# Residual by identity matmul, ScalarE copy and ScalarE's own queue for the last output piece

## The chip, the cores and the metric

The kernel runs on one core of one Trainium2 chip. The metric is the device time of one execution in microseconds (us). A profile gives the span of the core, from its first to its last instruction. This is about 2 us less than the device time.

## The reference, cut to what matters

Two layer types take turns, twice each, on x of 2048 rows by 1024 columns in bf16. The change touches the end of the last one:

```python
def _B_ref(x, w_gate, w_up, w_down):
    g = jnp.einsum("bsd,df->bsf", x, w_gate)
    u = jnp.einsum("bsd,df->bsf", x, w_up)
    h = g * u
    return jnp.einsum("bsf,fd->bsd", h, w_down)
...
x = x + _B_ref(_layernorm(x, axis=-1), B_w_gate, B_w_up, B_w_down)
```

The result is the residual x plus a down projection with an inner size of 3584. The kernel does this for 16 row tiles of 128 rows, each as a sum of 28 products of 128 by 128 weights (KF = 28).

## The kernel before

The residual lies in SBUF in `X`, in bf16, for all row tiles. Fifteen row tiles are finished whole (`d_unit`). The last is finished in three column pieces, so that only the small third piece has its addition and store after TensorE's last product:

```python
def add_store(t, a, b, ps, last):
    nc.vector.tensor_tensor(out=X[:, t, a:b], in0=X[:, t, a:b], in1=ps, op=ALU.add)
    if last:
        nc.sync.dma_start(out=o_view[:, t, a:b], in_=X[:, t, a:b])
...
def d_end(t):
    def run():
        tl = t % TPG
        for a, b in ((0, 512), (512, 896), (896, 1024)):
            ps = mm_tile()
            for f in range(KF):
                nc.tensor.matmul(out=ps[:, 0, 0:b - a], lhsT=hT[:, f, tl * P:(tl + 1) * P], rhs=wd[f][:, a:b],
                                 start=(f == 0), stop=(f == KF - 1))
            add_store(t, a, b, ps[:, 0, 0:b - a], True)
    return run
```

`mm_tile` hands out one of three accumulators in PSUM. `ident` is a 128 by 128 identity in bf16, made at the start for transposes. A pool of three small buffers (`eb`) is used by ScalarE's copies.

Of the kernel before, what the change touches and what calls it, by code (L numbers as in the profile page):

```python
# [11 lines left out]
BF16 = mybir.dt.bfloat16  # L12
# [14 lines left out]
def kernel(  # L27
# [11 lines left out]
    nc = tc.nc  # L39
    P = 128  # L40
    S, D = A_x.shape[1], A_x.shape[2]
# [3 lines left out]
    KF = F // P  # L45
# [10 lines left out]
    small = ctx.enter_context(tc.tile_pool(name="small", bufs=4))  # L56
# [8 lines left out]
    X = const.tile([P, NT, D], BF16, tag="X", name="X")  # L65
# [33 lines left out]
    o_view = out[0].rearrange("(t p) d -> p t d", p=P)  # L99
# [48 lines left out]
    ident = const.tile([P, P], BF16, tag="ident", name="ident")  # L148
# [6 lines left out]
    def mm_tile():  # L155
        return psum.tile([P, 2, NB], F32, tag="mm", bufs=3, name="ps")
# [388 lines left out]
# [4 lines that stand above are left out]
# [10 lines left out]
    def d_end(t):  # L559
        def run():  # L560
            tl = t % TPG
            for a, b in ((0, 512), (512, 896), (896, 1024)):
                ps = mm_tile()
                for f in range(KF):
                    nc.tensor.matmul(out=ps[:, 0, 0:b - a], lhsT=hT[:, f, tl * P:(tl + 1) * P], rhs=wd[f][:, a:b],  # L565
                                     start=(f == 0), stop=(f == KF - 1))
                add_store(t, a, b, ps[:, 0, 0:b - a], True)
        return run

    def do(units):  # L570
# [82 lines left out]
```

## Time and profile before

| | before |
|---|---|
| time, median of 3 runs (lowest to highest) | 1622.09 us (1621.53 to 1622.28) |
| span of the profiled run | 1620.1 us |
| TensorE busy | 1607.5 us, 99% |
| VectorE / ScalarE busy | 38% / 18% |
| end of TensorE's last product to end of span | some 2.65 us |

Read it from the end. The chain that ended last is TensorE's for 99% of the span, so nothing on another engine costs time unless TensorE waits for it, or it comes after TensorE's last product. The last three rows of the chain, in order of time (start, length, what):

```profile
1614.88 2.55 PE ps L565 x34
1617.44 0.02 issue
1617.46 0.29 DVE X L546
```

The add of 0.29 us is the only computation left after TensorE. The store and the closing barrier follow it.

### The profile page before, as it was taken

What the parts mean: (1) busy time and instruction counts of PE and PEld (TensorE: products, weight loads), DVE (VectorE), ACT (ScalarE), POOL (GpSimd) and SP (SyncE); (2) the same over time, 40 slices, a digit from 0 to 9 for tenths busy, and PEclk for the clock granted to TensorE, in tenths of its full rate; (3) what the DMA queues carried; (4) which work ended last, traced back from release to release, by engine and by line L of the source; (5) the groups of instructions that cost most, each with busy time, mean ns of one, the idle gap of its engine ahead of it and who ended that gap; (6) DMA issues with size and microseconds to landing.
All of it is one profiled execution on the core that took longest, in us unless ns stands there. A gap on an engine that the chain in (4) does not pass through costs nothing.

```text
span 1620.1 us, 18047 instructions
## 1 busy us (share of the span) xinstructions
PE 1607.5 (99%) x7710; PEld 734.5 (45%) x7861; DVE 616.6 (38%) x946; ACT 284.0 (18%) x384; POOL 54.5 (3%) x135
## 2 busy tenths in 40 slices
PE   9999999999999999999999999999999999999999
PEld 4444444444444444444444444444444444444444
DVE  6899853202311321243255798432123113211111
ACT  5522201101110110011045231011011101101110
POOL 2100000000000000010000000000000000000000
DMA  8224856512650552142420257655236306521400
GB/s 247 53 72 93 246 162 176 162 52 60 171 159 0 147 162 81 52 156 66 92 52 1 78 114 219 181 157 165 69 102 175 127 20 173 165 66 65 156 1 26
DMA packets 236719, 183.10 MB, mean 113 GB/s; under 512 B 102368, under 2 KB 217312, under 8 KB 236640
## 3 DMA queue, kind: packets, MB, share of 16 engines
q1 hardware_dynamic: 236640, 181.95, 39.0%
q8 instruction: 61, 1.00, 0.3%
q14 instruction: 18, 0.15, 0.0%
HBM read 153.09 MB, written 4.19 MB: 97 GB/s over the span
## 4 chain that ended last, share of the span: by engine, by line
PE 99%; issue 1%; DMA 0%; SPq 0%; DVE 0%
PE ps L196 50%; PE ps L538 48%; PE ps L565 1%; DMA W<-in_A_wqkv_dram 0%; PE kv L306 0%; SPq L109 0%; PE pm L328 0%; PE ps L328 0%; DVE X L546 0%
## 5 line engine op out<-in xcount | busy, mean ns | idle before, releaser
L538 PE MATMUL ps<-xT,R 128*128 128x512 bf16 x2382 | 525.9, 379 | 2.6
L538 PEld LDWEIGHTS <-R 128*128 128x128 bf16 x2432 | 238.0, 98 | 286.9
L542 DVE TENSOR_TENSOR R<-gs,ps 128x512 bf16<-128x512 f32 x224 | 153.9, 687 | 533.5 <-ACT gs L541 533.5
L196 PEld LDWEIGHTS <-R 128*128 128x128 bf16 x2248 | 220.0, 98 | 265.2
L541 ACT COPY gs<-ps 128x512 f32<-128x512 f32 x224 | 131.3, 586 | 1040.2 <-PE ps L538 1011.5
L538 PE MATMUL ps<-xT,W 128*128 128x512 bf16 x1130 | 250.4, 379 | 1.2
L196 PEld LDWEIGHTS <-xT 128*128 128x128 bf16 x1536 | 149.5, 98 | 181.4 <-issue 1.9
L196 PE MATMUL ps<-W,xT 128*128 128x512 bf16 x997 | 222.8, 379 | 1.9 <-issue 0.3
L538 PEld LDWEIGHTS <-W 128*128 128x128 bf16 x1152 | 112.7, 98 | 135.9
L196 PE MATMUL ps<-W,R 128*128 128x512 bf16 x733 | 170.1, 379 | 0.8
L546 DVE TENSOR_TENSOR X<-X,ps 128x1024 bf16<-128x1024 bf16 (+3 forms) x34 | 39.4, 1158 | 335.8 <-PE ps L196 282.8
L196 PE MATMUL ps<-R,R 128*128 128x512 bf16 x506 | 111.8, 379 | 0.4
L196 PE MATMUL ps<-PQ,R 128*128 128x512 bf16 x488 | 111.4, 379 | 0.5
L196 PE MATMUL ps<-R,xT 128*128 128x512 bf16 x502 | 110.3, 379 | 0.5
L201 ACT ACTIVATE e<-ps 128x1024 bf16<-128x1024 f32 x56 | 57.3, 1024 | 141.2 <-PE ps L196 86.0
L175 DVE BATCH_NORM_STATS2 st<-X 128x6 f32<-128x512 bf16 x128 | 81.7, 680 | 0.1
L179 POOL TENSOR_SCALAR ve<-mv 128x1 f32<-128x1 f32 x64 | 16.2, 254 | 1325.8 <-DVE mv L177 1325.8
L196 PE MATMUL ps<-GL,R 128*128 128x512 bf16 x240 | 57.8, 379 | 0.3
L196 PE MATMUL ps<-xT,R 128*128 128x512 bf16 x240 | 57.5, 379 | 0.2
L378 DVE TENSOR_TENSOR X<-X,ps 128x1024 bf16<-128x1024 bf16 x32 | 38.7, 1209 | 17.0 <-PE ps L196 17.0
L186 DVE TENSOR_SCALAR R<-X,mv,rstd 128x1024 bf16<-128x1024 bf16 x64 | 33.7, 542 | 27.3 <-POOL rstd L181 24.0
L205 DVE TENSOR_SCALAR e<-e 128x1024 bf16<-128x1024 bf16 x64 | 26.9, 421 | 38.1 <-ACT e L201 38.1
(73 smaller groups left out, 456.6 us busy)
## 6 DMA issues: line engine op xcount, KB each, us to landing
R<-in_B_w_gate_dram SPq DMA_DIRECT2D x38, 1024.0 KB, 5.4
R<-in_B_w_up_dram SPq DMA_DIRECT2D x38, 1024.0 KB, 7.6
W<-in_B_w_gate_dram SPq DMA_DIRECT2D x18, 1024.0 KB, 5.4
W<-in_B_w_up_dram SPq DMA_DIRECT2D x18, 1024.0 KB, 7.6
W<-in_A_wqkv_dram SPq DMA_DIRECT2D x10, 1024.0 KB, 6.2
W<-in_B_w_down_dram SPq DMA_DIRECT2D x6, 1024.0 KB, 11.2
X<-in_A_x_dram SPq DMA_DIRECT2D x16, 256.0 KB, 6.7
PQ<-in_B_w_down_dram SPq DMA_DIRECT2D x4, 1024.0 KB, 8.4
```

Of the source, the lines that this page charges most:

```text
L175: nc.vector.bn_stats(out=st[:, c, :], in_=X[:, t, c * NB:(c + 1) * NB])
L179: nc.gpsimd.tensor_scalar(out=ve[:], in0=mv[:, 1:2], scalar1=1e-5, scalar2=None, op0=ALU.add)
L186: nc.vector.tensor_scalar(out=dst, in0=X[:, t, :], scalar1=mv[:, 0:1], scalar2=rstd[:], op0=ALU.subtract, op1=ALU.mult)
L196: nc.tensor.matmul(out=ps[:, n, :], lhsT=lhsT, rhs=rhs[:, n * NB:(n + 1) * NB], start=start, stop=stop)
L201: nc.scalar.activation(out=e[:], in_=flat(ps), func=ACT.Exp, **sc)
L205: nc.vector.tensor_scalar(out=e[:], in0=e[:], scalar1=1.0, scalar2=EPS, op0=ALU.min, op1=ALU.add)
L378: nc.vector.tensor_tensor(out=X[:, t, :], in0=X[:, t, :], in1=flat(ps), op=ALU.add)
L538: nc.tensor.matmul(out=ps[:, n, :], lhsT=w[:, k, j * P:(j + 1) * P], rhs=xT[g % 2][:, k, :], start=(k == 0), stop=(k == KD - 1))
L541: nc.scalar.copy(out=gs[:], in_=ps[:, 0, :])
L542: nc.vector.tensor_tensor(out=hT[:, f, :], in0=gs[:], in1=ps[:, 1, :], op=ALU.mult)
L546: nc.vector.tensor_tensor(out=X[:, t, a:b], in0=X[:, t, a:b], in1=ps, op=ALU.add)
L565: nc.tensor.matmul(out=ps[:, 0, 0:b - a], lhsT=hT[:, f, tl * P:(tl + 1) * P], rhs=wd[f][:, a:b], start=(f == 0), stop=(f == KF - 1))
```

## The change

The intent is to shorten this tail. The residual of the third piece enters the accumulator through TensorE, so no addition is left; ScalarE, idle by then, takes the sum out; and the store is issued by the same engine, without a hand-over to SyncE. The result is rounded to bf16 once in both versions.

```diff
             for a, b in ((0, 512), (512, 896), (896, 1024)):
                 ps = mm_tile()
+                last = b == D
+                if last:
+
+                    nc.tensor.matmul(out=ps[:, 0, 0:b - a], lhsT=ident[:], rhs=X[:, t, a:b], start=True, stop=False)
                 for f in range(KF):
                     nc.tensor.matmul(out=ps[:, 0, 0:b - a], lhsT=hT[:, f, tl * P:(tl + 1) * P], rhs=wd[f][:, a:b],
-                                     start=(f == 0), stop=(f == KF - 1))
-                add_store(t, a, b, ps[:, 0, 0:b - a], True)
+                                     start=(f == 0 and not last), stop=(f == KF - 1))
+                if last:
+                    o = small.tile([P, P], BF16, tag="eb", bufs=3, name="o")
+                    nc.scalar.copy(out=o[:], in_=ps[:, 0, 0:b - a])
+                    nc.scalar.dma_start(out=o_view[:, t, a:b], in_=o[:])
+                else:
+                    add_store(t, a, b, ps[:, 0, 0:b - a], True)
```

## The prediction

> **What bounds the kernel now.** I read the page's list of busy engines first, then the chain that ended last, and then, because the change touches only the last 128 columns of the last row tile, the timeline, the waits and the issues of the last 16 us.
>
> ```profile
> span 1620.1 us, 18047 instructions
> PE 1607.5 (99%) x7710; PEld 734.5 (45%) x7861; DVE 616.6 (38%) x946; ACT 284.0 (18%) x384; POOL 54.5 (3%) x135
> PE 99%; issue 1%; DMA 0%; SPq 0%; DVE 0%
> PE ps L196 50%; PE ps L538 48%; PE ps L565 1%; DMA W<-in_A_wqkv_dram 0%; PE kv L306 0%; SPq L109 0%; PE pm L328 0%; PE ps L328 0%; DVE X L546 0%
> ```
>
> TensorE holds the chain from one end to the other. VectorE (38%), ScalarE (18%) and the transfers hang beside it. The changed function is the source line 565 group, 1% of the chain. So whatever is done to the last piece can only move what comes after TensorE's last product, plus any matmul put into its stream. The timeline of the end shows the size of that:
>
> ```profile
> 1615.70 0.61 PE L565 MATMUL ps<-PQ,R 128*128 128x128 bf16 x8
> 1615.90 0.56 DVE L546 TENSOR_TENSOR X<-X,ps 128x384 bf16<-128x384 bf16 x1 [3.86 <-PE ps L565]
> 1616.14 0.61 PE L565 MATMUL ps<-W,R 128*128 128x128 bf16 x8
> 1616.59 0.39 PE L565 MATMUL ps<-GL,R 128*128 128x128 bf16 x4
> 1616.81 0.39 PE L565 MATMUL ps<-W,R 128*128 128x128 bf16 x4
> 1617.04 0.39 PE L565 MATMUL ps<-xT,R 128*128 128x128 bf16 x4
> 1617.46 0.29 DVE L546 TENSOR_TENSOR X<-X,ps 128x128 bf16<-128x128 bf16 x1 [1.01 <-PE ps L565]
> ```
>
> Columns: start, duration, engine, line, operation, count, and the idle time ahead. The last matmul ends about 1617.43 (1617.04 + 0.39), the add runs 1617.46 to 1617.75 (it is 288 ns), and the store is issued at once. The views of the store and of the closing line read:
>
> ```profile
> 1617.78 0.33 SPq L548 DMA_DIRECT2D out_dram<-X  x1
> out_dram<-X SPq DMA_DIRECT2D x1, 32.0 KB, 1.5
> SPq L648 <- DMA out_dram<-X: 0.9, 1, 0.9
> L648 SPq EVENT_SEMAPHORE  x7: 17/28/28, 1618.2 to 1620.0; - x7
> ```
>
> Issue at 1617.78, landing 1.5 us later, near 1619.28. SyncE has by then waited 0.9 us for it, and the closing barrier takes the 0.8 us to 1620.1. The whole tail after TensorE is 1620.1 - 1617.43 = 2.67 us: 0.03 hop, 0.29 add, 0.03 hop, 1.5 store, 0.8 barrier (these make 2.65). It is 0.16% of the time. **Even removing the add entirely could not make a difference of 2%**, which is 32 us.
>
> **What the Trainium skill says.** *TensorE: Matmul & The Clock Gate*, "Back-to-back issue gap", gives an isolated warm 128-column matmul 134 cycles (55.8 ns at its 2.4 GHz), and about 81 ns where every matmul has its own weight load. The trace: 24 starts from 1615.70 to 1617.04 make 1.34/24 = 55.8 ns each, weight loads included. It agrees with the first number and not with the second, so I use 56 ns.
>
> *ScalarE: Activation LUTs*, "What ACT_TABLE_LOAD costs", gives 186 ns + 0.833 ns per column for an ACTIVATE with immediate scale and bias. In the trace a copy out of PSUM takes 586 ns for 512 columns (line 541) and 1012 ns for 1024 (line 296): slope 426/512 = 0.832, fixed part 160 ns. The slope agrees, the fixed part is 26 ns lower for a copy. At 128 columns the trace's fit gives 160 + 107 = 267 ns.
>
> *DMA: Bandwidth & Descriptors*, "Issuing engines are not separate DMA queues": transfers issued from different engines end on the same 16 DMA engines, and a second issuer saves only sequencer time. In the trace SyncE's issues take 0.33 us. The store before is issued at 1616.48, so SyncE is free at 1616.81, nearly 1 us before 1617.78. There was no queueing to save.
>
> Same page, "Latency and other measured facts": a fixed cost near 2 us, mostly the write's receipt. The four last stores agree in kind: 256, 128, 96 and 32 KB take 2.0, 1.7, 1.6 and 1.5 us. Size hardly matters, and the issuer doesn't change this part.
>
> **The change part by part.** The compiled orders of both kernels, side by side, show exactly these moves: TensorE gets one weight load and one matmul more, VectorE loses its last add, ScalarE gets a copy and a transfer issue at the end of its list, SyncE loses its last store. All else keeps its order.
>
> *Identity matmul.* It is one more 128-column matmul on the engine that sets the end, ahead of the 28 of the piece. Its weights are the identity made at the start, its moving operand the residual X. Its weight load overlaps the matmul before, as all do here. Cost: +0.056 us, all on the path. It carries the one wait on VectorE that the piece's first product carried before: this is the wait for a free accumulator, used three allocations earlier by row tile 14, whose add ends at 1605.30 + 1.22 = 1606.52, nine us before it is needed. X's columns 896 to 1024 of this tile were last written in the third layer.
>
> *Copy instead of add.* 267 ns against 288 ns: -0.02 us. The start should not move: in the trace VectorE's add starts 0.20 us after the next group's first matmul starts (1581.13 against 1580.93), and ScalarE's copy of the line 541 group also 0.20 us (1569.04 against 1568.84). ScalarE's last earlier work is that copy at 1569.04, so it is idle for 48 us and comes at once. Its destination is one of three small buffers whose last readers finished near 1570.
>
> *Issue from ScalarE.* Before, VectorE's semaphore releases SyncE 0.03 us after the add. After, ScalarE's own copy has to complete before ScalarE issues; the list still shows a wait on ScalarE's own count. So the hop is kept in another form: 0, give or take 0.05. The issue is taken as the same 0.33 us and the landing as the same 1.5 us, with no ScalarE issue in this trace to check it.
>
> *The end.* SyncE does its checks of earlier stores earlier, but the last landing still releases it, and the barrier's 0.8 us stay. The two VectorE releases that SyncE no longer handles cost nothing there.
>
> Sum: +0.056 - 0.021 + 0.0 = **+0.035 us**, so 1622.09 + 0.035 = 1622.1 us. That is a thirtieth of a microsecond, less than the 0.75 us between lowest and highest of the three runs before.
>
> **Rivals.** *(a) The identity matmul waits for the piece before.* If its read of X were tied to any write of X, it would wait for the add of columns 512 to 896, which ends at 1615.90 + 0.56 = 1616.46, while it could start at 1615.70: +0.8 us, 1622.9. Against it: at 1617.46 the last add writes X while the store of the columns beside it, issued at 1616.48 and taking 1.6 us, is still under way. So X is tracked by columns. I give this 5%.
>
> *(b) ScalarE's first transfer is dear.* Its queue is otherwise never used in this kernel. If first use, or a slower issue there, costs 0.2 to 1 us, the time is 1622.3 to 1623.1. For it: nothing in this trace measures a ScalarE issue, and SyncE's own first issues took about 0.43 us against 0.33 later. Chance of over 0.2 us: 20%.
>
> *(c) The hop really disappears and ScalarE issues sooner.* This would be the author's hope. What can vanish is at most the 0.03 us gap, and, if the issue's preparation overlaps the copy, perhaps 0.1 to 0.2 us: 1621.9. Chance: 25%.
>
> *(d) The tail is hidden anyway.* It is not: the chain ends in the add and the store, nothing runs beside it. Every ns of it counts, there are only few of them.
>
> **Range and chances.** The mechanisms span -0.2 to +1 us. The three runs before span 0.75 us, and a new set on perhaps another chip can sit some tenths elsewhere. I take 1620.9 to 1623.4, wider above for (a) and (b). For 2% the effect would have to be some forty times the largest rival, so nearly all the chance lies within.
>
> **What would show it.** In the trace after: a first 128-column matmul in the last piece reading X, with the 29 starts still 56 ns apart; if a gap of 0.8 us follows the 384-column group, (a) is right. A ScalarE copy of about 267 ns starting 0.03 us after the last matmul. A ScalarE issue of about 0.33 us starting within 0.05 us of the copy's end; if it is longer or its landing is over 1.7 us, (b). From last matmul to the end, 2.6 to 2.7 us. No last store on SyncE. My prediction would be wrong if the barrier at the end, or the start, grew with a second transfer queue in use, which no view of the kernel before can tell, or if the matmul stream lost its 100% granted clock.

## The result, and the profile after

| | before | after |
|---|---|---|
| time, median of 6 runs (lowest to highest) | 1621.95 us (1621.53 to 1622.28) | 1621.87 us (1621.65 to 1623.05) |
| ratio, 95% interval | | 1.0001 (0.9988 to 1.0013) |
| span of the profiled run | 1620.1 us | 1620.1 us |

A ratio is the mean time of one kernel's fast runs over that of the other's of the same rounds, so not quite the ratio of the medians.

The page after, its busy engines and its chain by engine:

```profile
PE 1607.7 (99%) x7711; PEld 734.5 (45%) x7862; DVE 616.2 (38%) x945; ACT 284.2 (18%) x385; POOL 54.3 (3%) x135
PE 99%; issue 1%; DMA 0%; SPq 0%; ACT 0%
```

One matmul more, one weight load more, one VectorE instruction less, one ScalarE instruction more: the change did what it says. The timeline of the end, after (start, duration, engine, line, operation, idle time ahead):

```profile
1615.67 0.22 PE L567 MATMUL ps<-X,ident 128*128 128x128 bf16 x1
1615.73 0.61 PE L569 MATMUL ps<-PQ,R 128*128 128x128 bf16 x8
1615.88 0.56 DVE L546 TENSOR_TENSOR X<-X,ps 128x384 bf16<-128x384 bf16 x1 [3.86 <-PE ps L569]
1617.07 0.39 PE L569 MATMUL ps<-xT,R 128*128 128x128 bf16 x4
1617.49 0.27 ACT L573 CAST o<-ps 128x128 bf16<-128x128 f32 x1 [47.89 <-PE ps L569]
1617.79 0.37 ACTq L574 DMA_DIRECT2D out_dram<-o  x1
```

The identity matmul starts at 1615.67 with no idle time noted ahead of it, while the add of the piece before is only about to start (1615.88): it did not wait for that add. The next product starts 0.06 us later. ScalarE's copy took the place of the add, 0.27 for 0.29 us, and its issue took 0.37 us where SyncE's took 0.33.

For so small a change the span is too coarse a measure, since the head of the kernel moves it more. I use two intervals inside the trace. **A** runs from the start of row tile 14's add, the last common event that the change can't reach (1605.30 before, 1605.28 after), to the start of the last store's issue. **B** runs from there to the trace's end stamp (1620.06 before, 1620.13 after).

| | A, us | B, us | A + B |
|---|---|---|---|
| before | 1617.78 - 1605.30 = 12.48 | 2.28 | 14.76 |
| after | 1617.79 - 1605.28 = 12.51 | 2.34 | 14.85 |

So the changed tail is about 0.09 us **longer**: 0.03 us in A, 0.06 us in B. The views round to 0.01 us. The stamps of the packed traces, in ns, give A 12.472 and 12.508 (+0.036), B 2.286 and 2.337 (+0.051). They also split B where SyncE sees that the last store has landed: up to there 1.467 and 1.505 us (+0.038), from there to the end 0.819 and 0.832 (+0.013). No timed comparison here could see that; the traces can, if they repeat.

### The profile page after: what moved, and what is told of

The parts are those of the page before. It is cut to its first block, busy times and chain, and to the rows that moved or that the text cites. A ratio compares the mean times of both kernels' runs of the same rounds, so it can differ in the third digit from the quotient of the medians.

```text
span 1620.1 us, 18050 instructions
## 1 busy us (share of the span) xinstructions
PE 1607.7 (99%) x7711; PEld 734.5 (45%) x7862; DVE 616.2 (38%) x945; ACT 284.2 (18%) x385; POOL 54.3 (3%) x135
## 4 chain that ended last, share of the span: by engine, by line
PE 99%; issue 1%; DMA 0%; SPq 0%; ACT 0%
PE ps L196 50%; PE ps L538 48%; PE ps L569 1%; DMA W<-in_A_wqkv_dram 0%; PE kv L306 0%; SPq L109 0%; PE pm L328 0%; PE ps L328 0%; ACT o L573 0%; PE ps L567 0%
## 5 line engine op out<-in xcount | busy, mean ns | idle before, releaser
L546 DVE TENSOR_TENSOR X<-X,ps 128x1024 bf16<-128x1024 bf16 (+2 forms) x33 | 39.1, 1185 | 334.8 <-PE ps L196 282.8
```

## The experiments

Theory after the result: A grew by the matmul (+0.056) less the faster copy (-0.02); B grew because ScalarE's issue is longer than SyncE's, by its nature or by its first use. Rivals: the moved hop, a wait of the identity matmul, or mere scatter between two traces. All kernels below gave correct results. In rows with several runs the time is compared with the kernel before, of the same session.

**The changed kernel once more** (no edit), for the scatter.

> The changed kernel once more, to see how far one trace of it repeats: last store issued 12.51 +- 0.02 us after row tile 14's add begins, its issue 0.37 us, 2.34 +- 0.04 us from there to the end. If these move by 0.05 us or more, the tail's differences read from single traces mean nothing.

Measured: tile 14's add starts at 1605.02, the last issue at 1617.53, the end stamp is 1619.87: A 12.51, B 2.34, sum 14.85, issue 373 ns. The tail repeats to 0.01 us. (The kernel before was traced once only.) The span was 1619.9 against 1620.1: all of this difference lies ahead of the last 15 us.

**The two parts of the change apart.** First, identity matmul and copy with SyncE's issue:

```diff
-                    nc.scalar.dma_start(out=o_view[:, t, a:b], in_=o[:])
+                    nc.sync.dma_start(out=o_view[:, t, a:b], in_=o[:])
```

> Identity matmul and ScalarE copy stay, the last store is issued by SyncE as before. My theory (three small terms that nearly cancel: +0.056 matmul, -0.02 copy, +0.04 us longer issue, the last one not on the path because the landing time is the same): issue 0.33 us instead of 0.37, copy's end to issue 0.03 us, landing 1.5 us, tail from the last matmul's start group to the end as in the changed kernel, span 1620.1 +- 0.3. Rival (the queue change saved a hop that hid a larger cost): the issue starts 0.1 us or more later after the copy's end than the 0.035 us of ScalarE's own issue, and the tail is longer by as much.

Measured: A 1618.25 - 1605.74 = 12.51, B 1620.54 - 1618.25 = 2.29. The copy starts at 1617.96 and takes 265 ns, so the issue comes 0.03 us after its end, as with ScalarE's own queue. **The hop that the change was to save costs the same within the same engine.** The longer B is gone with ScalarE's issue: 1.459 us up to the landing. The closing part after it is 0.832 us here too, so those 0.013 us don't belong to ScalarE's queue. My span of 1620.1 +- 0.3 missed (1620.5), because of the head, below. Secondly, VectorE's add with ScalarE's issue:

```diff
+                if last:
+                    add_store(t, a, b, ps[:, 0, 0:b - a], False)
+                    nc.scalar.dma_start(out=o_view[:, t, a:b], in_=X[:, t, a:b])
```

> VectorE's add of before stays (no identity matmul), only the last store is issued by ScalarE. My theory: 28 matmuls in the last piece, add 288 ns, ScalarE issue 0.37 us beginning 0.03 us after the add, landing 1.5 us; span 1620.1 +- 0.3. Rival (ScalarE issues sooner only because the copy is its own): the issue starts 0.1 us or more after the add's end.

Measured: add 286 ns, A 1617.25 - 1604.77 = 12.48 as before, issue 0.37 us, B 1619.59 - 1617.25 = 2.34 as after. So the two halves are separate: matmul and copy make A's 0.03 us, ScalarE's issue makes B's 0.06. Here too the span missed its forecast (1619.6), to the other side.

**Where the spans differ.** The first 11 us of TensorE show it. Before, at its first wait for a load:

```profile
10.24 12.03 PE L196 MATMUL ps<-W,xT 128*128 128x512 bf16 x54 [0.22 <-DMA W<-in_A_wqkv_dram]
```

In the run with SyncE's issue:

```profile
6.30 0.59 PE L196 MATMUL ps<-W,xT 128*128 128x512 bf16 x2 [0.56 <-DMA W<-in_A_wqkv_dram]
10.68 11.60 PE L196 MATMUL ps<-W,xT 128*128 128x512 bf16 x52 [0.28 <-DMA W<-in_A_wqkv_dram]
```

The first weight arrived late and TensorE stood 0.56 us at 6 us, which it didn't before; from there to the end it was 0.44 us behind (10.68 against 10.24, and 1605.74 against 1605.30). Arrival of the first loads differs between executions and moves the whole program. It is several times what the change does.

**Is a matmul wholly on the path, and at which price?** 41 identity matmuls, each overwriting the one before:

```diff
-                    nc.tensor.matmul(..., rhs=X[:, t, a:b], start=True, stop=False)
+                    for c in range(41):
+                        nc.tensor.matmul(..., rhs=X[:, t, a:b], start=True, stop=(c < 40))
```

> 41 identity matmuls instead of one, each overwriting the one before (result unchanged). My theory: every one lies wholly on the path at 56 ns, so the last piece's matmuls take 40 x 0.0558 = 2.23 us more, the span is 2.2 us longer, and the time about 1624.2 us (ratio 1.0014). Rival (a weight load ahead of each makes it dearer, 81 ns or more, or part of it is hidden): 3.2 us more, or clearly under 2 us.

```profile
1615.62 2.45 PE L568 MATMUL ps<-X,ident 128*128 128x128 bf16 x41
1617.85 1.61 PEld L570 LDWEIGHTS <-R 128*128 128x128 bf16 x28
1617.90 0.61 PE L570 MATMUL ps<-PQ,R 128*128 128x128 bf16 x8
1619.67 0.27 ACT L574 CAST o<-ps 128x128 bf16<-128x128 f32 x1 [50.12 <-PE ps L570]
```

From the first identity matmul to the first product 1617.90 - 1615.62 = 2.28 us, or 2.28/41 = 55.6 ns each, every one with its own weight load. A is 1619.96 - 1605.22 = 14.74, 2.23 more than in the changed kernel, the forecast to 0.01 us. The time was 1624.21 us against 1621.76 (ratio 1.0015, 1.0002 to 1.0027): +2.45 us, where the trace sums say 14.74 + 2.34 - 14.76 = 2.32. Nothing of a matmul here is hidden.

**Did the identity matmul wait for the neighbouring piece?** A second one ahead of it reads 64 columns that the add of the piece before writes:

```diff
+                    nc.tensor.matmul(out=ps[:, 0, 0:b - a], lhsT=ident[:], rhs=X[:, t, a - 64:b - 64], start=True, stop=True)
                     nc.tensor.matmul(out=ps[:, 0, 0:b - a], lhsT=ident[:], rhs=X[:, t, a:b], start=True, stop=False)
```

> A second identity matmul ahead of the first reads columns 832 to 960 of the residual, of which 832 to 896 are written by the add of the piece before; the next one overwrites its result, so the output stays right. My theory (the residual is tracked by columns, so the changed kernel's matmul waited for nothing): here TensorE stands still until that add ends, 0.75 to 0.85 us after the 384-column group, plus 0.056 us for the matmul; span +0.8 to +0.9 us. Rival (the wait is there already in the changed kernel or costs nothing): no gap, span +0.06 us.

The chain of this run around the piece:

```profile
1614.94 0.83 PE ps L570 x5
1615.77 0.02 issue
1615.80 0.57 DVE X L546
1616.36 0.04 issue
1616.40 0.22 PE ps L567
```

Now the add of the piece before is in the chain, and TensorE stands still until it ends. A is 1618.57 - 1605.20 = 13.37, 0.86 more than in the changed kernel; the time was 1622.72 us (1622.65 to 1622.75) against 1621.74, +0.98. In the changed kernel this wait does not exist. It also shows what a carelessly chosen slice of the residual would have cost: ten times the change.

**Does the tail have anything beside it?** The copy done nine times over:

```diff
-                    nc.scalar.copy(out=o[:], in_=ps[:, 0, 0:b - a])
+                    for _ in range(9):
+                        nc.scalar.copy(out=o[:], in_=ps[:, 0, 0:b - a])
```

> The ScalarE copy is done nine times over the same tiles. My theory: the tail has nothing beside it, so all of the eight more copies show in the time: 8 x 0.265 = 2.1 us if they don't overlap, 8 x 0.17 = 1.4 us if each overlaps the one before by some 0.09 us; time 1623.3 to 1624.1. Rival (the tail is hidden by earlier stores or by the closing work): under 0.5 us.

```profile
1619.27 2.65 ACT L574 CAST o<-ps 128x128 bf16<-128x128 f32 x9 [47.89 <-PE ps L569]
1621.94 0.37 ACTq L575 DMA_DIRECT2D out_dram<-o  x1
```

All of it shows: A is 1621.94 - 1607.06 = 14.88, 2.37 more than in the changed kernel. My size missed: the copies start (2.65 - 0.27)/8 = 0.30 us apart, more than their own 0.265, so there is no overlap but a gap between them. The packed trace shows that each of the eight later copies waits on ScalarE's own semaphore (semaphores are the counters by which engines wait for work to be done). All nine write one tile, so this is presumably the wait for the copy before; the run therefore says nothing about copies that don't wait. The time was 1624.51 us (1624.13 to 1627.13) against 1621.76. B is 2.52 us, because the closing part after the landing took 1.00 instead of 0.83 us; why, and the wide range, I leave unexplained. In the profiled run another 1.8 us lay in the head: among other things eight transposes took 1.04 instead of 0.62 us there, and the 512-column products started 0.43 instead of 0.22 us apart until 9.8 us.

**Is ScalarE's issue longer by nature or by first use?** In the changed kernel all three stores of the last tile go to ScalarE:

```diff
-                    add_store(t, a, b, ps[:, 0, 0:b - a], True)
+                    add_store(t, a, b, ps[:, 0, 0:b - a], False)
+                    nc.scalar.dma_start(out=o_view[:, t, a:b], in_=X[:, t, a:b])
```

> Changed kernel, but the stores of the 512 and 384 column pieces are issued by ScalarE as well, so that the last issue is the third on that queue. Theory A (ScalarE's issue is simply longer, 0.37 against 0.33 us): all three of its issues take about 0.37 us, the last lands after 1.5 us. Theory B (the 0.04 us is a cost of first use): the first takes 0.37 or more, the last 0.33.

Measured: the three issues took 375, 338 and 339 ns in this order, and SyncE's last issue before had taken 332. The first one on ScalarE's queue is the longest. B fell to 1620.75 - 1618.44 = 2.31. But A rose to 12.57, because the copy came late. To part the two, only the first of the pieces was moved:

```diff
-                    add_store(t, a, b, ps[:, 0, 0:b - a], True)
+                    add_store(t, a, b, ps[:, 0, 0:b - a], a > 0)
+                    if a == 0:
+                        nc.scalar.dma_start(out=o_view[:, t, a:b], in_=X[:, t, a:b])
```

> The changed kernel with only the 512-column piece's store moved to ScalarE, 5 us ahead of the last one. Theory (the 37 ns longer issue is a cost of first use, and the late copy of the three-issue run came from the issue directly ahead of it): first issue 0.375, last issue 0.338 us, copy starts 0.42 us after the start of the last group of four matmuls as in the changed kernel, last store issued 12.51 us after row tile 14's add begins, and from there to the end 2.30 us instead of 2.34. Rival (length by chance): last issue 0.37 us again.

```profile
L578 ACTq DMA_DIRECT2D out_dram<-X x1: 375/375/375, 1612.2 to 1612.2; - x1
L574 ACTq DMA_DIRECT2D out_dram<-o x1: 338/338/338, 1618.0 to 1618.0; - x1
```

Issues of 375 and 338 ns again, B 1620.32 - 1618.02 = 2.30. Over all runs ScalarE's first store took 368 to 383 ns (ten traces), its later ones 338 or 339 (three issues in two traces). This fits first use. It is not all that makes an issue long: in the trace before SyncE's 18 stores took 332 to 361 ns, none of them the first on its queue, and the 64-column run below has one of 382. The copy is late again, though, by 0.05 us and with the other issue 5 us back, so my reason for it (an issue directly ahead) fell. The end of the chain of this run shows another:

```profile
1616.07 1.58 PE ps L569 x28
1617.65 0.02 issue
1617.67 0.02 ACTq L573
1617.68 0.04 issue
1617.72 0.27 ACT o L573
```

Between TensorE's last product and the copy stands an instruction of ScalarE's sequencer, a semaphore wait of 17 ns on the copy's line, with 0.02 and 0.04 us around it. In the changed kernel that wait stands at 1569.0, long before. The compiled lists tell why: there the copy waits for VectorE and for TensorE, and the first, long satisfied, is passed early; with an earlier store in ScalarE's list the copy waits for TensorE and for ScalarE's own count. The packed traces name the semaphores and bear this out. In the changed kernel the separate wait is on VectorE's (number 105) and the copy itself waits on TensorE's (100). Here the separate wait, at 1617.67, is on TensorE's, and the copy itself waits on ScalarE's own (110). What is won in B (0.04) is lost in A (0.05).

**What does the width of the last piece do?** The kernel before with two pieces of 512:

```diff
-            for a, b in ((0, 512), (512, 896), (896, 1024)):
+            for a, b in ((0, 512), (512, 1024)):
```

> The kernel before, with the last row tile in two pieces of 512 columns instead of three: the last add is 512 wide. My theory: 28 matmul overheads fewer (28 x 2.5 ns = -0.07 us), add 0.687 instead of 0.288 (+0.40), store of 128 KB lands after 1.7 instead of 1.5 us (+0.2): span +0.5 us, time 1622.5. It shows that the width of the last piece matters an order of magnitude more than who empties it. Rival: the same tail, no change.

Measured: the last add starts at 1617.48 and takes 689 ns, A is 12.81 (+0.33, as summed: 0.40 - 0.07), B is 2.59 (+0.31; the store lands after 1.7 instead of 1.5 us). The time was 1622.44 us (1622.36 to 1622.58) against 1621.76 (1621.61 to 1621.95): +0.68, where the traces say 0.64; the ranges don't touch, though the interval of the ratio (0.9991 to 1.0018) holds 1. The 0.07 us are 28 times 2.5 ns, which can be worked out from the trace before: the 384-column products start (1615.70 - 1611.15)/28 = 162.5 ns apart, the 128-column ones 55.8; this makes 0.417 ns a column and some 2.5 ns for each product. Then narrower, `(0, 512), (512, 960), (960, 1024)`:

> The kernel before with its last two pieces cut at column 960: the last add is 64 wide. Theory A (matmul starts are N/2.4 GHz + 2.5 ns apart down to 64 columns): the products cost the same in sum, the add takes 0.22 instead of 0.29 us, and the last store is issued 0.07 us sooner after row tile 14's add (12.41 instead of 12.48 us): it would beat both kernels by that much. Theory B (with its own weight load a matmul can't start less than some 50 ns after the one before): 28 x 25 ns = 0.7 us more on TensorE, and 0.6 us slower in all.

```profile
1616.61 0.40 PE L565 MATMUL ps<-PQ,R 128*128 128x64 bf16 x8
1617.31 0.28 PE L565 MATMUL ps<-xT,R 128*128 128x64 bf16 x4
1617.62 0.22 DVE L546 TENSOR_TENSOR X<-X,ps 128x64 bf16<-128x64 bf16 x1 [0.20 <-PE ps L565]
```

24 starts in 0.70 us are 29 ns each: theory A for the matmuls. The add took 220 ns, as summed, and A was 12.41, as theory A had it. A first reading gave 12.46: it took the last issue to be 0.33 us long, as in the kernel before, counted back from its end to a start at 1617.93, and concluded that SyncE's queue was in the way. That was wrong, as two views of the issues show:

```profile
1617.45 0.81 SPq L548 DMA_DIRECT2D out_dram<-X  x2
L548 SPq DMA_DIRECT2D out_dram<-X x2: 332/357/382, 1617.5 to 1617.9; - x2
```

The two issues end at 1617.45 + 0.81 = 1618.26. The first is the one of 332 ns and ended at 1617.79; the last took 382 ns and so started at 1617.88, 0.035 us after the add's end at 1617.845. SyncE was free 0.06 us before it was needed. What is longer is the issue itself, 382 against 332 ns, on a queue long in use; what makes it so is not known. B is 1620.21 - 1617.88 = 2.33, and A + B 14.74, only 0.02 us under before. The time was 1621.96 us (1621.70 to 1622.08) against 1621.66 (1621.49 to 1621.86), ratio 1.0001 (0.9985 to 1.0018). Two further runs were made on the strength of the wrong reading, which their expectations repeat. The first has ScalarE issue the last store:

```diff
-                add_store(t, a, b, ps[:, 0, 0:b - a], True)
+                add_store(t, a, b, ps[:, 0, 0:b - a], b < D)
+                if not (b < D):
+                    nc.scalar.dma_start(out=o_view[:, t, a:b], in_=X[:, t, a:b])
```

> As the run with the 64-column last piece (VectorE adds all three pieces), but the last store is issued by ScalarE. There, SyncE had ended its issue of the 112 KB piece only 0.06 us before the last add ended, and the last issue began 0.09 us after that add. Theory (SyncE's queue was the hindrance): here the last issue begins 0.03 us after the add, 12.40 us after row tile 14's add begins, takes 0.37 us (first use), and the end comes 2.34 us after its start. Rival (the gap belongs to the add): 0.09 us again, 12.46.

Measured: A 1618.38 - 1605.97 = 12.41, issue 369 ns, starting 0.03 us after the add, B 1620.70 - 1618.38 = 2.32. Both intervals are those of SyncE's issue (12.41 and 2.33): in A there was nothing to win. Theory and rival both rested on the wrong start, and both fell; that 12.40 was nearly met says nothing for the theory. The second has ScalarE issue the piece before (`a != 512` in place of `b < D`):

> 64-column last piece, VectorE adds, the 448-column piece stored by ScalarE and the last by SyncE: SyncE is free and its queue long in use. Theory (the terms add): last issue 12.40 us after row tile 14's add begins, 0.33 us long, the end 2.28 us after its start, so 14.68 us from that add to the end against 14.76 before and 14.85 changed: the shortest tail of all. In the time this is 0.08 us and not resolvable. Rival: a second queue costs at the end whatever it is used for: 2.34 us to the end again.

Measured: A 1617.89 - 1605.48 = 12.41, B 1620.20 - 1617.89 = 2.31 and not 2.28. The sum is 14.72, the shortest of all: 0.04 us under before, 0.13 under the change, 0.02 under the same pieces with both stores on SyncE. The time does not show it: 1622.23 us (1622.12 to 1622.37) against 1621.85 (1621.36 to 1622.35), ratio 1.0003 (0.9986 to 1.0019). I don't call it a faster kernel. For the 0.03 us in B neither theory gives an account: the issue itself was the short one (332 ns). One half is the closing part (0.833 against 0.819), the other the way to the landing (1.480 against 1.467); differences of this size are seen in the other traces with either issuer.

## Why the prediction was right or wrong

**The bound: right.** TensorE's chain stayed at 99%, and the change acted on a tail of 2.7 us. The forecast of 1622.1 us stands against 1621.87, within the stated range. This proves little of the mechanism: the times of all the rivals (1621.9 to 1623.1) lie within the range as well, and only the traces tell them apart. (A slip without effect: 32 us is forty times the 0.8 us of rival (a), but 32 times the 1 us of rival (b).)

**The identity matmul, +0.056 us with nothing hidden: right.** Its product follows 0.06 us later; 41 of them cost 55.6 ns each. Together with the copy it was to lengthen A by 0.035 us; by the stamps in ns it was 0.036.

**The copy, 267 ns against 288: right.** It was 265 ns, starting 0.02 us after the last product in the chain, as the add did. The fit from wider copies of the trace held at a quarter of the smallest width it came from.

**The hop, "kept in another form", 0 +- 0.05 us: right.** 0.03 us in both forms, shown by the run with SyncE's issue.

**The issue from ScalarE, "taken as the same 0.33 us": the term that was mis-sized.** It was 0.37 us, and B grew by 0.06 (0.051 by the stamps in ns). The sum was to be +0.035 us and was +0.09. Of B's growth 0.038 us lie before the landing, as much as the issue is longer (0.037), and are gone where SyncE issues; the other 0.013 lie in the closing part and are still there where SyncE issues, so they are not the queue's. Rival (b) had named first use or a slower issue, but set it at 0.2 to 1 us; it is 0.04 us. Two runs with an earlier issue fit first use; why some of SyncE's issues are as long is open.

**Rival (a), a wait on the neighbouring columns, 5%: rightly thrown out.** Forced, it costs the 0.8 us that were computed. **Rival (c), a shorter hop: not seen in any run**, the 64-column ones included: the last issue began 0.03 to 0.04 us after the add or copy with either issuer. **Rival (d): rightly thrown out**; nine copies showed in full.

**"My prediction would be wrong if the barrier at the end, or the start, grew with a second transfer queue":** nothing of the kind beyond the 0.06 us was found at the end. At the start, spans scatter by more than the change with either kernel.

## What to carry to other kernels

First size the part that the change can reach: a tail of 2.7 us in 1620 can't give 2%, however well it is rebuilt, and here none of the three moves bought anything: a matmul of 0.056 us went in to save 0.02 at the copy, a hop of 0.03 was exchanged for another of 0.03, and an issue of 0.33 for one of 0.37. Measure such a change between two events inside the trace, close around it, and repeat one trace to learn the scatter; the span and the time carry the noise of the kernel's first loads. Whether a second issuing engine helps where the first is still busy when the last store becomes ready was not tested: in every version here SyncE was free by then. And read an issue's start from a view that shows its own length, not by counting back with the length of another.

## What the Trainium skill lacked or had wrong

- *TensorE: Matmul & The Clock Gate*, "Back-to-back issue gap": it gives about 81 ns for 128-column matmuls in a stream with weight loads. Here they start 55.6 to 55.8 ns apart, each with its own weight load (41 identity matmuls, 24 products), which is its figure for isolated ones. Its table has about 60 cycles at 64 columns, 25 ns at its 2.4 GHz; 24 starts were 29 ns apart, which is what the formula of the same section, N/2.4 + 2.5, gives (29.2).
- *ScalarE: Activation LUTs*, "What ACT_TABLE_LOAD costs": it gives 186 ns + 0.833 ns per column for an ACTIVATE, which would be 293 ns for 128 columns, and names no figure for a copy. The copy out of PSUM, a CAST in the trace, took 265 ns. Its overlap of some 93 ns between back-to-back instructions is not refuted by the nine copies, of which the eight later ones waited on ScalarE's own semaphore; in the trace before an instruction of 1.11 us from 20.80 and the next, from 21.81, overlap by 0.10 us.
- *DMA: Bandwidth & Descriptors*: no section tells that the first issue on an engine's queue is longer. It was 368 to 383 ns for ScalarE's first, 338 and 339 for its later ones, 332 for SyncE's last; but SyncE's last was once 382, so first use is not the only thing that lengthens one.
- *Perfetto Trace Analysis*, "Identifying Dependency Chains", says that an instruction which waits for several engines may get EventSemaphore instructions ahead of it. It doesn't say that an earlier store in the engine's list can change which of the waits is the separate one, nor what that costs; here it made the copy 0.05 us later.
